# The last group's small pass evicted by two engines, and its two closings split between them

## The chip, the cores and the metric

The kernel runs on one core of a Trainium2 chip. The core has a matrix engine (TensorE, PE in the profile, with its weight loads shown apart as PEld), a vector engine (VectorE, DVE), a scalar engine (ScalarE, ACT), a general engine (GpSimd, POOL) and a queue engine (SyncE, SP). They run side by side, each working through its own instructions in order, and wait for each other by semaphores. Matmuls write into PSUM, an accumulator memory used here as eight banks of 512 floats per partition; ScalarE and VectorE move results from there to the main on-chip memory ("eviction"). The metric is the device time of one execution in microseconds, lower is better.

## The reference

```python
# attention part: a causal convolution of 7 taps along the sequence, softmaxed weights per head
w = softmax(weight, axis=-1)                        # 8 heads x 7 taps
out[b, s, h, g] = sum_k w[h, k] * x_pad[b, s + k, h, g]
# channel part, x = out, D = 192, hidden width 4 * 192 = 768
xn = (x - mean) / sqrt(var + 1e-6) * g_ln
y = x + relu(xn @ w_ch1) @ w_ch2
```

Shapes are x: 8 x 4224 x 192 in float32; the result has the same shape.

## The kernel before

Rows are cut into 18 groups (two small ones first); a full group is 128 partitions x 16 rows of 192 channels. For every group VectorE and ScalarE compute the convolution, VectorE transposes it in 32x32 blocks, and TensorE does the *up* stage (192 to 768, then relu) and the *down* stage (768 to 192). The normalisation's mean is folded into the weights, and its scale (`rstd`, computed by GpSimd) is applied after the down stage.

From group 3 on the up stage is `up_mixed`, which saves matmuls: it does a 2x2 block product with seven products instead of eight (Strassen-like), and adds and subtracts blocks around them. Its hidden features are cut in two passes. The *small* pass `one` covers one of three feature blocks (`n == 1`, 24 matmuls in a product, 1,024 results per partition); the *large* pass `two` covers the other two (`PAIR = 2`, 48 matmuls, 2,048 results). Two sets of four PSUM banks, X and Y, take turns: while TensorE fills one, the other is read. A product begins only when the earlier contents of its set have been read out. Within a bank, the columns hold `f` (which feature block of the pass, 256 columns each); `q` is the bank in the set.

Two helpers read a set. `evict` (L640 to L642) copies or rectifies it on ScalarE. `close` (L644 to L652) adds it to a block `c` that was evicted earlier: either VectorE adds directly from PSUM (L648), or ScalarE copies the set to a spare part and a DMA on GpSimd's queue adds that part to `c` (L609, by `add_by_dma`).

In a group that is not the last, pass two closes c11 in two halves by `f`, each by a ScalarE copy and a DMA, and c22 in one piece in the same way; VectorE is busy there with the next group's convolution. In the last group there is no next group, so both are closed by VectorE as a whole. c21 is closed by VectorE in every group.

`next(ahead)` between the two passes emits the finish of the previous group on VectorE (`finish_fast`, L897 and L899: sums and block transposes of the previous down stage into the tile `ot`). In the last group two scalings of that tile by `rstd` follow on VectorE (L709), each followed by two DMAs that add to the output (L925). `down_fast` then starts with products over c11, c21 and c22; its results are read by ScalarE (L841).

The order of the work is written by hand: each engine executes in the order of emission, and a framework inserts the semaphores that the data and the PSUM banks need.

Of the kernel before, what the change touches and what calls it, by code (L numbers as in the profile page):

```python
# [10 lines left out]
AF = mybir.ActivationFunctionType  # L11
ALU = mybir.AluOpType
# [4 lines left out]
def kernel(  # L17
# [29 lines left out]
    nc = tc.nc  # L47
# [35 lines left out]
    PAIR = NF // 2 - 1  # L83
    HJ = J // 2
# [9 lines left out]
    def rows_of_out(g, j1, j2):  # L94

        b, j0, n = groups[g]
        if b is not None:
            return [(slice(0, P), outr[b, :, (j0 + j1) * D : (j0 + j2) * D])]
        left = out[:, P * R : S].rearrange("b (p r) d -> b p (r d)", p=LP)
        return [  # L100
            (slice(LP * b, LP * b + LP), left[b, :, j1 * D : j2 * D]) for b in range(B)
        ]
# [22 lines left out]
    def take_set():  # L125
        i = (turn[0] + 3) // 4 * 4 % 8
        turn[0] = i + 4
        return all_banks[:, i : i + 4]
# [357 lines left out]
    def store_y(g, queue=nc.sync):  # L486
        n = groups[g][2]
        for ps, rows in rows_of_out(g, 0, n):
            queue.dma_start(out=rows, in_=y[g][ps, 0:n].rearrange("p j d -> p (j d)"))
# [118 lines left out]
    def add_by_dma(dst, src):  # L608
        nc.gpsimd.dma_start(out=dst, in_=src, accum_op=ALU.add)  # L609

    def up_mixed(g, ahead, pending):
# [3 lines left out]
        last = g + 1 == NG  # L615
# [7 lines left out]
        class Pass:  # L623
# [15 lines left out]

            def evict(self, banks, dst, relu=False, f=None):  # L640
                src = self.seen(banks, f)
                nc.scalar.activation(dst, src, AF.Relu) if relu else nc.scalar.copy(dst, src)  # L642

            def close(self, c, banks, part=None, f=None):  # L644


                if part is None:
                    nc.vector.tensor_tensor(c, c, self.seen(banks), op=ALU.add)  # L648
                    return
                self.evict(banks, part, f=f)  # L650
                whole = "p f q w -> p (f q w)"
                add_by_dma(c.rearrange(whole), part.rearrange(whole))  # L652
# [4 lines left out]
        def parts(pool, tag):  # L657

            room = pool.tile([P, J * D], F32, tag=tag, name=f"parts_{tag}{g}")
            return room.rearrange("p (f q w) -> p f q w", q=NQ, w=W)  # L660

        def act_scales(j1, j2):
            if not last:
                scale(g - 1, j1, j2)

        def taps_of_next(*args, **kw):
            if not last:
                conv(g + 1, *args, **kw)


        X, Y = take_set(), take_set()
        one, two = Pass(PAIR, FC, X, Y), Pass(0, PAIR, Y, X)
        p = one
# [18 lines left out]
        p = two  # L692
        rooms = parts(cpool, "cs"), parts(bpool, "tb")
        p.product(Y, a11, p.b11, True, False)
        p.evict(Y, p.c11)
        p.product(X, a12, p.b21)
        if last:
            p.close(p.c11, X)
        else:
            for f in range(PAIR):  # L700
                p.close(p.c11[:, f : f + 1], X, rooms[0][:, f : f + 1], f)
            if g == 3:
                store_y(g, nc.gpsimd)
        act_scales(0, 1)
        if last:

            for j1 in (0, HJ):
                part, factor = ots[g - 1][:, j1 : j1 + HJ], rstd[g - 1][:, j1 : j1 + HJ]
                nc.vector.tensor_tensor(  # L709
                    part, part, factor.unsqueeze(2).to_broadcast([P, HJ, D]), op=ALU.mult  # L710
                )
                add_to_out(g - 1, j1, j1 + HJ)
        p.product(Y, s2, p.t[0], False, False)
        p.evict(Y, p.c21)
        one.relu(one.c11)
# [3 lines left out]
        p.product(Y, s1, p.b12, False, False)  # L719
        taps_of_next(2, 5)  # L720
        taps_of_next(5, 6, heads=(0, H // 2))
        p.close(p.c22, Y, None if last else rooms[1][:, 0:PAIR])
        p.product(X, a22, p.t[2], False)
        for f in range(PAIR):
            p.relu(p.c11[:, f : f + 1])
# [8 lines left out]
        p.product(Y, s4, p.b22, False)  # L734
        p.evict(Y, p.c12, True)
        if last:
            p.relu(p.c22)
        lower_sum(g, range(PAIR))
        if last:

# [65 lines left out]
    def lower_sum(g, fs=range(FC)):  # L806

        a = of_products(g)
        if g in MIXED:
            for f in fs:  # L810
                nc.vector.scalar_tensor_tensor(
                    out=a[:, 1, 0, f], in0=a[:, 1, 0, f], scalar=0.0, in1=a[:, 0, 0, f],
                    op0=ALU.max, op1=ALU.subtract,
                )
        else:
            half_sum(g, (1, 0), (1, 0), (0, 0), ALU.subtract, fs)
# [99 lines left out]
    def add_to_out(g, j1, j2):  # L916
        if groups[g][0] is None:

            j1, j2 = (0, j2) if j2 == groups[g][2] else (0, 0)
        for ps, rows in rows_of_out(g, j1, j2) if j2 else ():  # L920
            src = ots[g][ps, j1:j2].rearrange("p j d -> p (j d)")
            step = 4 * D if groups[g][0] is not None else (j2 - j1) * D
            for d0 in range(0, (j2 - j1) * D, step):
                d1 = min(d0 + step, (j2 - j1) * D)
                nc.gpsimd.dma_start(out=rows[:, d0:d1], in_=src[:, d0:d1], accum_op=ALU.add)  # L925
# [65 lines left out]
    for g in range(NG):  # L991
        mixed, last = g in MIXED, g + 1 == NG
        if g + 2 < NG and g not in (1, 2, 3):
            load_x(g + 2)
        if mixed:
            work = up_mixed(g, ahead(g), pending)
            pending = iter(())
        else:
            up(g)
            work = []  # L1000
# [90 lines left out]
```

## Time and profile before

| | us |
|---|---|
| median of 4 runs | 957.55 |
| lowest, highest | 956.03, 958.65 |
| profiled execution, its own time | 957.56 |
| its span, first to last instruction | 955.5 |
| TensorE matmuls busy | 947.3 (99%) |
| VectorE busy | 891.0 (93%) |
| ScalarE busy | 696.6 (73%) |
| GpSimd busy | 336.9 (35%) |
| last group, small pass (weight loads) | 894.49 to 904.11 |
| last group, large pass | 904.11 to 922.78 |

A busy TensorE is not TensorE at its peak, since matmuls overlap; its weight loads show better when it had to wait. In a timeline row the first number is the start in us from the start of the span, the second the time from the first instruction of the row to the end of its last, then engine, source line, operation, what is written and read, the shape and the number of instructions; in brackets is the idle time of the engine before the row and what ended it.

### The profile page before, as it was taken

Reading aid. Unit: us, or ns where it says so; the run is one execution under the profiler, and the core shown is the slowest. Engines: PE = TensorE matmul, PEld = TensorE weight load, DVE = VectorE, ACT = ScalarE, POOL = GpSimd, SP = SyncE. Lnnn points to the kernel's source line nnn. Section 1 sums busy time; section 2 is a strip of 40 time slices with the busy share of each in tenths; the row PEclk is TensorE's granted clock in tenths of the full one; section 3 lists DMA queues with packets and bytes.
Section 4 is the critical chain, followed back from the end, with each engine's and each line's share of the span. In section 5 each row is a group of like instructions: output and inputs, shape, how many; then the busy total and the mean of one; then the engine's idle time right before and its main releaser. Section 6 shows DMA issues by size and latency. Waiting matters only on the chain.

```text
span 955.5 us, 37878 instructions
## 1 busy us (share of the span) xinstructions
PE 947.3 (99%) x16858; PEld 735.9 (77%) x16858; DVE 891.0 (93%) x1489; ACT 696.6 (73%) x1165; POOL 336.9 (35%) x472
## 2 busy tenths in 40 slices
PE   8999999999999999999999999999999999999998
PEld 6998896876869687787968778695877869586787
DVE  7999999999999999999999999999999999999757
ACT  6753678596877959687795968779696877967462
POOL 1158422623145141533227141442316332261310
PEclk9999999999999999999999999999999999999999
DMA  8359589689797988979697896969889696778251
GB/s 207 105 155 216 103 227 279 120 186 229 135 266 138 245 163 186 220 132 276 122 254 152 192 221 128 275 132 251 157 193 213 129 274 133 175 135 139 43 95 67
DMA packets 39544, 168.82 MB, mean 177 GB/s; under 512 B 4437, under 2 KB 8150, under 8 KB 33367
## 3 DMA queue, kind: packets, MB, share of 16 engines
q0 software_dynamic: 32576, 106.25, 60.0%
q1 hardware_dynamic: 6800, 60.16, 17.2%
q8 instruction: 132, 2.16, 0.9%
q14 instruction: 30, 0.25, 0.1%
q10 hardware_dynamic: 6, 0.00, 0.0%
HBM read 38.93 MB, written 50.33 MB: 93 GB/s over the span
## 4 chain that ended last, share of the span: by engine, by line
PE 97%; DVE 1%; DMA 1%; SPq 0%; issue 0%; ACT 0%; DVEq 0%
PE ps L533 49%; PE ps L835 44%; PE ps L772 4%; DMA xg<-in_x_dram 1%; DVE y L417 1%; DVE yt L428 0%; SPq L220 0%; SPq L215 0%; PE ps L357 0%; PE ps L354 0%; SPq L168 0%; ACT y L380 0%; DVE y L929 0%; DVEq L417 0%; DVEq L428 0%
## 5 line engine op out<-in xcount | busy, mean ns | idle before, releaser
L417 DVE SCALAR_TENSOR_TENSOR y<-xg,taps,y 128x384 f32<-128x384 f32 (+3 forms) x720 | 365.0, 581 | 3.3 <-DMA y<-room 1.4
L835 PE MATMUL ps<-room,w2sums 128*32 128x256 f32 (+2 forms) x4608 | 247.3, 371 | 0.0
L533 PE MATMUL ps<-yt,w 32*128 32x256 f32 (+2 forms) x4104 | 234.8, 378 | 1.0 <-DVE yt L428 1.0
L642 ACT COPY room<-ps 128x1024 f32<-128x1024 f32 (+1 forms) x135 | 175.0, 1297 | 77.8 <-PE ps L533 77.8
L533 PEld LDWEIGHTS ps<-yt,w 32*128 32x128 f32 x4104 | 204.1, 185 | 26.4 <-issue 9.0
L835 PEld LDWEIGHTS ps<-room,w2sums 128*32 128x32 f32 x4608 | 150.6, 110 | 90.6 <-ACT room L655 5.0
L835 PE MATMUL ps<-room,w 128*32 128x256 f32 (+2 forms) x3456 | 189.4, 371 | 0.0
L802 DVE TENSOR_TENSOR room<-room 128x1024 f32<-128x1024 f32 (+2 forms) x147 | 161.2, 1169 | 22.9 <-PE ps L835 15.0
L835 PEld LDWEIGHTS ps<-room,w 128*32 128x32 f32 x3456 | 112.0, 110 | 69.1 <-DVE room L648 5.0
L533 PE MATMUL ps<-ysums,w1sums 32*128 32x256 f32 x2160 | 125.3, 379 | 0.2 <-issue 0.2
L533 PEld LDWEIGHTS ps<-ysums,w1sums 32*128 32x128 f32 x2160 | 109.1, 185 | 11.2 <-ACT room L642 3.6
L925 POOL DMA_DIRECT2D out_dram<-ot x69 | 59.0, 942 | 159.0 <-ACT ot L914 102.3
L409 POOL DMA_DIRECT2D y<-tb x59 | 52.5, 1386 | 154.2 <-ACT room L841 110.2
L841 ACT COPY cs<-ps 128x256 f32<-128x256 f32 (+2 forms) x192 | 70.2, 368 | 45.3 <-PE ps L835 45.2
L655 ACT ACTIVATE room<-room 128x1024 f32<-128x1024 f32 (+1 forms) x89 | 92.6, 1072 | 1.0 <-DMA room<-parts_cs 1.0
L914 ACT ACTIVATE ot<-ot,r 128x192 f32<-128x192 f32 x224 | 91.0, 465 | 0.0
L380 ACT ACTIVATE y<-xg,taps 128x384 f32<-128x384 f32 (+3 forms) x141 | 73.1, 608 | 1.1 <-DMA xg<-in_x_dram 1.1
L448 DVE BATCH_NORM_STATS2 st<-y 128x6 f32<-128x192 f32 x264 | 70.1, 343 | 0.0
L841 ACT COPY room<-ps 128x256 f32<-128x256 f32 (+2 forms) x96 | 35.5, 369 | 46.2 <-PE ps L835 44.2
L398 ACT ACTIVATE tb<-xg,taps 128x384 f32<-128x384 f32 (+1 forms) x120 | 66.0, 628 | 0.0
L533 PE MATMUL ps<-yt,w1sums 32*128 32x256 f32 x1080 | 65.2, 380 | 0.0
L533 PE MATMUL ps<-ysums,w 32*128 32x256 f32 x1080 | 64.6, 376 | 0.0
(113 smaller groups left out, 911.0 us busy)
## 6 DMA issues: line engine op xcount, KB each, us to landing
xg<-in_x_dram SPq DMA_DIRECT2D x14, 2112.0 KB, 16.8
room<-room POOLq DMA_DIRECT2D x45, 512.0 KB, 5.1
out_dram<-ot POOLq DMA_DIRECT2D x59, 384.0 KB, 9.6
y<-tb POOLq DMA_DIRECT2D x58, 384.0 KB, 9.0
out_dram<-y SPq DMA_DIRECT2D x13, 1536.0 KB, 9.2
room<-parts_cs POOLq DMA_DIRECT2D x28, 512.0 KB, 6.8
room<-parts_tb POOLq DMA_DIRECT2D x14, 1024.0 KB, 7.6
xg<-in_x_dram POOLq DMA_DIRECT2D x1, 2112.0 KB, 13.5
```

What stands on the lines that cost most here:

```text
L380: nc.scalar.mul(y[g][:, 0:n, cs], xg[g][:, 0:n, cs], taps[:, h, 0:1])
L398: nc.scalar.mul(tb[g][:, 0:n, cs], xg[g][:, 1 : 1 + n, cs], taps[:, h, 1:2])
L417: nc.vector.scalar_tensor_tensor(out=y[g][:, 0:n, cs], in0=t[:, k : k + n, cs], scalar=taps[:, h, k : k + 1], in1=y[g][:, 0:n, cs], op0=AL ...
L448: nc.vector.bn_stats(out=sums[g][:, j, :], in_=y[g][:, j, :])
L533: nc.tensor.matmul(banks[:, q, i * w : i * w + w], right[rows, c, P * i : P * i + P], left[rows, :, c, :], start=(first and c == 0 and i = ...
L642: nc.scalar.activation(dst, src, AF.Relu) if relu else nc.scalar.copy(dst, src)
L655: nc.scalar.activation(c, c, AF.Relu)
L802: nc.vector.tensor_tensor(a[:, *dst, f], a[:, *left, f], a[:, *right, f], op=op)
L835: nc.tensor.matmul(dst[C * q : C * q + C, 0:w], right[:, f, C * c : C * c + C], left[:, f, q], start=(first and f == PAIR), stop=(f == PAI ...
L841: nc.scalar.copy(to[:, c], dst[:, 0:w].rearrange("p (j t) -> p j t", t=t))
L914: nc.scalar.mul(ots[g][:, j, :], ots[g][:, j, :], rstd[g][:, j : j + 1])
L925: nc.gpsimd.dma_start(out=rows[:, d0:d1], in_=src[:, d0:d1], accum_op=ALU.add)
```

## The change

Only the last group is touched. In pass `one`, each eviction is cut by banks: ScalarE takes banks 0 and 1 of the set, VectorE banks 2 and 3. In pass `two`, c11 and c22 are each closed in two halves by `f`: the first by VectorE's sum from PSUM, the second by a ScalarE copy into a part of `rooms[1]` and a DMA that adds it. The four output DMAs of the previous group are issued after the closing of c22 instead of after each scaling. The final rectification of c22 is cut in two by `f`.

```diff
             def evict(self, banks, dst, relu=False, f=None):
                 src = self.seen(banks, f)
+                if last and self.n == 1:
+                    near, far = [[v[:, :, q : q + 2] for v in (dst, src)] for q in (0, 2)]
+                    if relu:
+                        nc.scalar.activation(*near, AF.Relu)
+                        nc.vector.tensor_scalar_max(*far, 0.0)
+                    else:
+                        nc.scalar.copy(*near)
+                        nc.vector.tensor_copy(*far)
+                    return
                 nc.scalar.activation(dst, src, AF.Relu) if relu else nc.scalar.copy(dst, src)
...
                 if part is None:
-                    nc.vector.tensor_tensor(c, c, self.seen(banks), op=ALU.add)
+                    nc.vector.tensor_tensor(c, c, self.seen(banks, f), op=ALU.add)
                     return
...
         p.product(X, a12, p.b21)
-        if last:
-            p.close(p.c11, X)
-        else:
-            for f in range(PAIR):
-                p.close(p.c11[:, f : f + 1], X, rooms[0][:, f : f + 1], f)
-            if g == 3:
-                store_y(g, nc.gpsimd)
+        for f in range(PAIR):
+            part = (rooms[1][:, 0:1] if f else None) if last else rooms[0][:, f : f + 1]
+            p.close(p.c11[:, f : f + 1], X, part, f)
+        if g == 3:
+            store_y(g, nc.gpsimd)
         act_scales(0, 1)
         if last:
...
                 nc.vector.tensor_tensor(
                     part, part, factor.unsqueeze(2).to_broadcast([P, HJ, D]), op=ALU.mult
                 )
-                add_to_out(g - 1, j1, j1 + HJ)
...
-        p.close(p.c22, Y, None if last else rooms[1][:, 0:PAIR])
+        if last:
+            for f in range(PAIR):
+                p.close(p.c22[:, f : f + 1], Y, rooms[1][:, f : f + 1] if f else None, f)
+            for j1 in (0, HJ):
+                add_to_out(g - 1, j1, j1 + HJ)
+        else:
+            p.close(p.c22, Y, rooms[1][:, 0:PAIR])
...
         if last:
-            p.relu(p.c22)
+            for f in range(PAIR):
+                p.relu(p.c22[:, f : f + 1])
```

Lines of the changed kernel stand 9 to 13 higher in its profile: `close`'s sum is L657 there, ScalarE's copies L648 and L651, the finish L910 and L912.

## The prediction

> **What bounds the kernel now.** I read the page's busy shares and chain first, then the weight loader's timeline in the last group (its starts give TensorE's pace), then the timelines of ScalarE and VectorE in the same stretch, then the DMA issues.
>
> ```profile
> PE 947.3 (99%) x16858; PEld 735.9 (77%) x16858; DVE 891.0 (93%) x1489; ACT 696.6 (73%) x1165; POOL 336.9 (35%) x472
> PE 97%; DVE 1%; DMA 1%; SPq 0%; issue 0%; ACT 0%; DVEq 0%
> ```
>
> 97% of the chain that ends last is matmul time, so only holes in TensorE's stream are to be won or lost. Those of the last group's up stage (start in us, duration, idle time before it and its releaser):
>
> ```profile
> 894.49 2.47 PEld L533 LDWEIGHTS ps<-yt,w 32*128 32x128 f32 x48 [0.41 <-issue]
> 897.20 1.18 PEld L533 LDWEIGHTS ps<-ysums,w1sums 32*128 32x128 f32 x24 [0.24 <-ACT room L642]
> 901.34 1.18 PEld L533 LDWEIGHTS ps<-yt,w1sums 32*128 32x128 f32 x24 [0.26 <-ACT room L642]
> 904.11 5.06 PEld L533 LDWEIGHTS ps<-yt,w 32*128 32x128 f32 x96 [0.22 <-ACT room L642]
> 909.18 2.58 PEld L533 LDWEIGHTS ps<-ysums,w1sums 32*128 32x128 f32 x48
> 912.05 2.47 PEld L533 LDWEIGHTS ps<-ysums,w1sums 32*128 32x128 f32 x48 [0.29 <-DVE room L648]
> 914.53 2.58 PEld L533 LDWEIGHTS ps<-ysums,w 32*128 32x128 f32 x48
> 917.12 2.58 PEld L533 LDWEIGHTS ps<-yt,w1sums 32*128 32x128 f32 x48
> 919.98 2.47 PEld L533 LDWEIGHTS ps<-yt,w 32*128 32x128 f32 x48 [0.28 <-DVE room L648]
> ```
>
> The small pass (7 products of 24 matmuls) runs from 894.49 to 904.11, 9.62 us, with three waits for a ScalarE eviction. The large pass waits 0.29 us for VectorE's closing of c11 and 0.28 us for that of c22. Unhindered, 48 matmuls take 2.59 us (914.53 to 917.12), so 24 take 1.295.
>
> The two evicting engines there:
>
> ```profile
> 896.14 1.01 ACT L642 COPY room<-ps 128x1024 f32<-128x1024 f32 x1 [1.13 <-PE ps L533]
> 916.75 2.95 ACT L655 ACTIVATE room<-room 128x1024 f32<-128x1024 f32 x3
> 922.92 1.88 ACT L642 ACTIVATE room<-ps 128x2048 f32<-128x2048 f32 x1 [3.22 <-PE ps L533]
> 926.49 0.97 ACT L841 COPY cs<-ps 128x192 f32<-128x192 f32 x4
> ```
>
> ```profile
> 888.94 1.07 DVE L875 TENSOR_TENSOR cs<-cs,ps 128x256 f32<-128x256 f32 x3
> 895.97 0.94 DVE L897 TENSOR_TENSOR cs<-cs,room 128x768 f32<-128x768 f32 x1
> 899.79 1.90 DVE L899 STREAM_TRANSPOSE ot<-cs 128x512 f32<-128x512 f32 x3
> 909.71 2.29 DVE L648 TENSOR_TENSOR room<-room,ps 128x2048 f32<-128x2048 f32 x1 [8.02 <-PE ps L533]
> ```
>
> What to see: VectorE finishes the group before (L897, L899) from 895.97 to 901.69, in 5.72 us, and then idles 8.02 us until c11's closing. That idle time is where the change puts work. The DMAs of this part (median us from issue to landing):
>
> ```profile
> room<-room POOLq DMA_DIRECT2D x3, 512.0 KB, 4.6
> out_dram<-ot POOLq DMA_DIRECT2D x4, 384.0 KB, 8.2
> ```
>
> **The change part by part**, against the profiled execution: span 955.5 us, its own time 957.56, so 2.06 lie around the span; the median of the four runs, 957.55, is the same. All products stay and TensorE's order is unchanged, and so is every group but the last.
>
> *1. Small pass.* Each eviction of 1,024 elements becomes 512 on ScalarE and 512 on VectorE, in different banks. ScalarE's copies take 0.37 us for 256 (L841) and 1.01 for 1,024, so 0.59 for 512. VectorE has no copy out of PSUM in this trace; its sums out of PSUM take 0.41 us alone for 256 (groups view of L875) and 2.29 for 2,048, on a line 0.68 for 512. A set's products come two apart: with the loader ready 0.24 us before 897.20, an eviction that begins at 896.14 may last about 0.8 us before TensorE waits. 0.68 fits, 1.01 did not. At 1.295 a product the pass lasts 9.07 instead of 9.62: **−0.55** at most, 0 if VectorE's copy is as slow as the present one. I take −0.52, as 0.68 is nearer the sums' rows; the large pass begins at 903.59. The new waits of TensorE on VectorE go to separate queue entries; the trace has such entries in this line at 51 ns, beside matmuls. I take 0 (bounds 0 and 8 x 0.05 = 0.4).
>
> *2. What queues behind VectorE's halves.* The finish of the group before stands behind the seven halves in VectorE's order. Its 5.72 us no longer start at 895.97 but after the last half, at 904.35 − 0.52 + 0.68 = 904.51, and end at 910.23. The idle 8.02 us are used up. Who waits: c11's closing, due at 909.71 − 0.52 = 909.19. It starts 1.06 us late.
>
> *3. c11's closing.* The sum of 2,048 on VectorE (2.29) becomes a sum of 1,024 there and a copy of 1,024 on ScalarE that a DMA adds. The halves are the left and right columns of the *same* four banks. The built kernel's instruction list shows ScalarE's two such copies each waiting on VectorE, so I count them in series: a sum of 1,024 is 1.19 (the line from 0.41 to 2.29), then 1.01. Hence 910.25 to 911.44, then 911.5 to 912.5, and TensorE goes on with s3·t1 at 912.55. It would be ready at 909.18 − 0.52 + 2.58 = 911.24: a wait of 1.3 us for the 0.29 of before. Against 912.05 the stream now stands at **+0.5**; the small pass's gain is spent. Were the halves side by side, it would go on at 911.5, and the stream stand at −0.55.
>
> Here a page bears on it. The Trainium skill, "PSUM — Partial Sum Buffer", section "PSUM bank collisions raise a hardware error", says the compiler's scheduler keeps any two engines apart that touch the same bank and partition quadrant, reads against reads included. No row of before shows two engines reading one bank. By the rule the sum is the serial one (+0.5); by the 128x1024 and 128x2048 rows read as if both engines were free, it is −0.55.
>
> *4. c22's closing.* VectorE is free (after c11 come the two scalings, 3.42 us, to 914.9). Half a sum from 917.64 + 0.5 = 918.14 to 919.33, then ScalarE's copy to 920.4. TensorE, ready at 917.12 + 0.5 + 2.58 = 920.2, starts s4·b22 at 920.45 for 919.98 before: the wait is 0.25 instead of 0.28, **−0.03**. Side by side it would be 0.
>
> *5. Behind that copy on ScalarE.* Three rectifications (2.95 us) move from 916.75 to 920.4 and end at 923.35. Next is c12's eviction, due at 922.92 + 0.47 = 923.39, which TensorE waits for in its first product of the down stage (0.29 us at 924.85 in before). It just fits: 0, with 0.04 us of cover; each further tenth of delay costs a tenth. One of the three needs c11's DMA: issued at about 912.5, landing 4.6 us later by the median row and 9.3 by the slowest of the other parts' rows (parts_cs, 4.5 to 9.3), so at 917 to 922; needed at about 921.5. Taken as 0.
>
> *6. c22's second rectification* needs the new DMA, issued at 920.4, landing at 925.0 by the median (6.0 is the slowest of its kind here: 926.4; 9.3: 929.7). The single 1.90 us becomes two of about 1.05, ending at 927.4. The four copies behind (0.97) end at 928.4; the last frees the bank that the product of c22 overwrites at about 929.1 (144 matmuls from 925.69 in 5.82, half of it, plus 0.47). Cover 0.7 us; taken as 0, with +0.4 at a landing 7.1 us after issue as the point where it begins.
>
> *7. Outputs of the group before* move behind both part DMAs in POOL's queue: issued from 921.3 instead of 913.97. Four issues of 0.87 and 9.9 us at most to land (that line's slowest) end at about 934; their tile is next written at 941.09. Cover 7 us; nothing is queued behind them on POOL. SP's queue is not touched. 0. The two added part DMAs cost POOL 0.87 us each, hidden, since it then only waits.
>
> Sum: −0.52 + 1.02 (c11) − 0.03 = **+0.47**, so 957.56 + 0.5 = 958.0 us.
>
> **Rivals.**
> - *A. The halves of a closing run side by side* (the waits on VectorE release early). c11 leaves −0.55, c22 −0.28: 956.7 us. For it: both engines have room there. Against: the waits listed in 3.
> - *B. The small pass gains nothing* (VectorE's copies about 0.9 us, or queue entries count), while the late finish stays: +1.0, 958.6 us. Against: the sums' rows, 1.05 ns an element.
> - *C. Slower side: c22's DMA lands late.* With the outputs behind it or a slow landing of 9.3 us, it is there at 929.7; rectification and copies end at 931.7, and TensorE waits 2.6 us at 929.1: 958.0 + 2.6 = 960.6. It decides from 7.1 us after issue. For it: parts_cs has a median of 6.8. Against: those go two at once beside other traffic; here the three lone ones took 4.5, 4.6 and 6.0.
> - *D. The change does nothing* within the noise: every gain and loss is a few tenths, so this cannot be told from the forecast.
>
> **How the numbers follow.** Forecast 0.62, A 0.10, B 0.16, C 0.12. What a measurement of this kernel can tell from no change is about 0.2%, 1.9 us: faster means under 955.6, slower over 959.5. Forecast, A and B all lie within, C over. The four runs of before spread from 956.03 to 958.65, about 1.3 us to either side, which adds small chances beyond both bounds. Faster 0.03, same 0.83, slower 0.14. The range goes from A less a little spread (956.3) to between B and C (959.8).
>
> **What would show it.** Weight loads of the small pass with no wait for ScalarE and the large pass beginning near 903.6; L910 and L912 from about 904.5 instead of 895.97; VectorE's first half closing near 910.3; ScalarE's parts_tb copies starting just after VectorE's halves end; a wait of about 1.3 us of TensorE before s3·t1; c12's eviction at about 923.4 with next to no idle time before it; the lone part DMAs landing after 4.5 to 6 us. It would be wrong if ScalarE's and VectorE's halves overlap, if VectorE's finish starts early, or if TensorE waits in the down stage for a DMA.

## The result and the profile after

The changed kernel takes 958.86 us (median of 40 runs, 957.2 to 960.94) against 957.51 (60 runs of the kernel before, 955.52 to 959.79): a ratio of 1.0016 with a 95% interval of 1.0011 to 1.0020, so it is slower by about 1.5 us (1.1 to 1.9). The profiled execution took 959.24 us with a span of 957.0, before 957.56 with 955.5. The forecast was 958.0 in a range of 956.3 to 959.8, with 83% on "same", a change of less than about 0.2%; the measured 0.16% is inside both.

Executions differ by a few tenths to two us before the last group begins, in code that the change does not touch (the small pass's first weight load stands at 894.49 in before, at 894.98 in after, and between 892.62 and 895.77 in the experiments). So places in the last group are compared from that first load on. The weight loader's timeline in the changed kernel:

```profile
894.98 2.47 PEld L533 LDWEIGHTS ps<-yt,w 32*128 32x128 f32 x48 [0.41 <-issue]
897.47 2.58 PEld L533 LDWEIGHTS ps<-ysums,w1sums 32*128 32x128 f32 x48
902.65 6.46 PEld L533 LDWEIGHTS ps<-yt,w 32*128 32x128 f32 x120
909.12 2.58 PEld L533 LDWEIGHTS ps<-ysums,w1sums 32*128 32x128 f32 x48
912.89 2.47 PEld L533 LDWEIGHTS ps<-ysums,w1sums 32*128 32x128 f32 x48 [1.19 <-ACT parts_tb L651]
920.79 2.47 PEld L533 LDWEIGHTS ps<-yt,w 32*128 32x128 f32 x48 [0.26 <-ACT parts_tb L651]
923.60 1.78 PEld L848 LDWEIGHTS ps<-room,w 128*32 128x32 f32 x48 [0.33 <-DVE room L657]
932.36 0.29 PEld L848 LDWEIGHTS ps<-room,w 128*32 128x32 f32 x7
933.56 2.54 PEld L848 LDWEIGHTS ps<-room,w 128*32 128x32 f32 x64 [0.91 <-issue]
945.34 7.77 PEld L785 LDWEIGHTS ps<-w,kept 128*128 128x128 f32 x48 [0.30 <-issue]
```

The same two places of the down stage in the kernel before, the product that has the hole above and the first load of the kept rows:

```profile
931.54 2.89 PEld L835 LDWEIGHTS ps<-room,w 128*32 128x32 f32 x72
943.51 7.77 PEld L772 LDWEIGHTS ps<-w,kept 128*128 128x128 f32 x48 [0.30 <-issue]
```

Three things are to be seen. The small pass has no wait for ScalarE any more. The wait before s3·t1 has grown from 0.29 to 1.19 us and names ScalarE's copy. And there is a hole of 0.91 us in the down stage, after 7 loads of a product, where the loader waited for nothing that the profile shows ("issue"); the kernel before has no such hole there. From the first load, s3·t1 stands at 17.91 us (before 17.56), s4·b22 at 25.81 (25.49), the down stage at 28.62 (28.29) and the first load of the kept rows at 50.36 (49.02). That last stretch (called "the stretch" below) is 1.34 us longer: 0.33 in the up stage, 1.01 in the down stage.

How the late start of s3·t1 comes about, in VectorE's and then ScalarE's timeline of the changed kernel:

```profile
904.43 0.69 DVE L646 TENSOR_SCALAR room<-ps 128x512 f32<-128x512 f32 x1 [0.60 <-PE ps L533]
905.03 0.95 DVE L910 TENSOR_TENSOR cs<-cs,room 128x768 f32<-128x768 f32 x1
908.79 1.90 DVE L912 STREAM_TRANSPOSE ot<-cs 128x512 f32<-128x512 f32 x3
910.61 1.18 DVE L657 TENSOR_TENSOR room<-room,ps 128x1024 f32<-128x1024 f32 x1
918.47 1.22 DVE L657 TENSOR_TENSOR room<-room,ps 128x1024 f32<-128x1024 f32 x1 [3.35 <-PE ps L533]
```

```profile
904.37 0.60 ACT L645 ACTIVATE room<-ps 128x512 f32<-128x512 f32 x1 [0.65 <-PE ps L533]
911.82 1.01 ACT L651 COPY parts_tb<-ps 128x1024 f32<-128x1024 f32 x1 [2.97 <-DVE room L657]
919.73 1.01 ACT L651 COPY parts_tb<-ps 128x1024 f32<-128x1024 f32 x1 [1.99 <-DVE room L657]
923.74 1.88 ACT L651 ACTIVATE room<-ps 128x2048 f32<-128x2048 f32 x1
```

VectorE ends its last half eviction at 905.1, then finishes the group before, and starts c11's half at 910.61 with no idle time. ScalarE sits idle for 2.97 us and begins its half of c11 just after VectorE's ends (910.61 + 1.18 = 911.79). The two halves run one after the other, in c22 as well.

### The profile page after: what moved, and what is told of

It reads as the page before. It is cut to its first block, busy times and chain, and to the rows that moved or that the text cites. A ratio compares the mean times of both kernels' runs of the same rounds, so it can differ in the third digit from the quotient of the medians.

```text
span 957.0 us, 37896 instructions
## 1 busy us (share of the span) xinstructions
PE 949.1 (99%) x16858; PEld 738.1 (77%) x16858; DVE 893.1 (93%) x1496; ACT 695.8 (73%) x1168; POOL 340.9 (36%) x474
## 4 chain that ended last, share of the span: by engine, by line
PE 66%; DVE 1%; issue 0%; ACT 0%; DVEq 0%
PE ps L848 34%; PE ps L533 31%; PE ps L785 1%; DVE ot L912 0%; DVE cs L910 0%; DVE room L657 0%; ACT parts_tb L651 0%; DVE y L942 0%; DVE room L646 0%; DVEq L912 0%
## 5 line engine op out<-in xcount | busy, mean ns | idle before, releaser
L651 ACT COPY room<-ps 128x1024 f32<-128x1024 f32 (+1 forms) x129 | 168.9, 1310 | 72.3 <-PE ps L533 72.0
L664 ACT ACTIVATE room<-room 128x1024 f32<-128x1024 f32 x90 | 92.6, 1062 | 0.8 <-DMA room<-parts_cs 0.6
```

The source lines that it names most:

```text
L664: nc.scalar.activation(c, c, AF.Relu)
```

## The experiments

After the result two causes stood for the 1.5 us. *Up stage*: the late finish and the halves in series, worth 0.3. *Code*: the hole of 0.91 us. It lies where the four output DMAs now fill the DMA engines, and TensorE's code comes over the same engines: the trace shows packets of 16,384 bytes in the queue marked "instruction". That they are TensorE's is inferred from their number and pace: the page counts 132 of them for 16,858 matmuls, one for about 128, and where a matmul takes 40 ns without disturbance (e5 below) they come every 5.0 to 5.2 us, about 128 matmuls. In this part of the changed kernel they start at 914.03, 921.89, 931.30 and 934.74; the gap of 9.4 us opens with the first packets of the part and the outputs (922.5) and ends some 3 us before their last (934.5). The DMA queues of the changed kernel from 926 to 934 us:

```profile
q0 software_dynamic: 547, 1.49, 99.0%
q8 instruction: 1, 0.02, 0.8%
```

(packets, MB, share of 16 engines.) The traffic does not slow the loads as such: the 144 loads ahead of the hole take 5.82 us beside it, as in the kernel before. The rival was that the hole belongs to the new code or to c22's halves. Times and durations below that have no fence are read from the same traces.

Ratios are against runs of the kernel before made alongside. Those of e1, e3, e4, e5, e7 and e8 all have 1.000 within their intervals, so what these runs say of a few tenths of a microsecond rests on the stretch, read from one profiled execution each. The kernel before and e1, which moves the outputs alone, agree on it to 0.01 us.

**e1: the late outputs alone, in the kernel before.**

```diff
-                add_to_out(g - 1, j1, j1 + HJ)
...
         p.close(p.c22, Y, None if last else rooms[1][:, 0:PAIR])
+        if last:
+            nc.gpsimd.tensor_copy(wmax[:, 0:1], p.c22[:, 0, 0, 0:1])
+            for j1 in (0, HJ):
+                add_to_out(g - 1, j1, j1 + HJ)
```

> The kernel before, with one edit: the four output DMAs of the group before the last are issued behind the closing of c22 (held back by a one-element copy on GpSimd that reads c22) instead of behind the scalings. Theory (the outputs now crowd the DMA engines while TensorE's code is fetched, and TensorE runs out of code in the down stage): outputs issued from about 920.2 instead of 914.0, a 16 KB instruction packet delayed by 3 to 4 us, a hole of 0.5 to 1.0 us marked issue in the weight loads of the down stage, time about 0.9 us over before (ratio 1.0005 to 1.001). Rival (the outputs' place costs nothing, the whole 1.5 us is in the evictions and closings): no hole, ratio 1.000.

Measured: 956.92 us, ratio 0.9993 (0.9983 to 1.0003), stretch 49.02 us as in before, and no hole. The outputs were issued at 921.50, in place of 913.97, and the code packets were 922.36 and 930.68, 8.3 us apart. So the outputs' late place delays the packet but is not enough for a hole. This went against my expectation; the table behind e5 shows what else it takes.

**e2: the changed kernel with the outputs back behind the scalings.**

```diff
+                add_to_out(g - 1, j1, j1 + HJ)
...
-            for j1 in (0, HJ):
-                add_to_out(g - 1, j1, j1 + HJ)
```

> The changed kernel with the output DMAs back behind the two scalings. Theory (code fetch behind the outputs): the up stage stays as in the changed kernel (s4*b22 25.8 us after the small pass's first load), the hole of 0.91 us in the down stage goes, time 0.9 us under the changed kernel, about 958.0. The added DMA of c22 now stands behind the outputs and lands later than its 5.1 us; from about 6.5 us on ScalarE's rectification and then TensorE wait for it, which would give back up to 1 us. Rival (the hole comes from something else in the down stage, such as c22's halves): the hole stays, 958.9.

Measured: 959.88 us, ratio 1.0024 (1.0013 to 1.0035), stretch 51.16 us. The hole is gone, as the theory had it, but the price that it named only as a possibility is larger than the gain. ScalarE's timeline and the weight loader's:

```profile
928.98 1.06 ACT L664 ACTIVATE room<-room 128x1024 f32<-128x1024 f32 x1 [2.84 <-DMA room<-parts_tb]
```

```profile
930.95 2.76 PEld L847 LDWEIGHTS ps<-room,w2sums 128*32 128x32 f32 x72 [1.97 <-ACT cs L853]
```

c22's part DMA, issued at 920.62 behind the outputs (issued from 913.33 to 917.12), lands after 8.3 us instead of 5.1; the second rectification of c22 waits 2.84 us for it, the copies behind it come late, and TensorE waits 1.97 us for a bank. That is the mechanism of the prediction's rival C, with the outputs in front of the part instead of behind it. The total of the forecast for this run (958.0) was wrong by it.

**e3: the closings halved by banks instead of columns.**

```diff
+            def close_by_banks(self, c, banks, part):
+                src = self.seen(banks)
+                near, far = c[:, :, 0:2], c[:, :, 2:4]
+                nc.vector.tensor_tensor(near, near, src[:, :, 0:2], op=ALU.add)
+                part = part.rearrange("p o q w -> p (o q w)")
+                nc.scalar.copy(
+                    part.rearrange("p (f q w) -> p f q w", f=PAIR, w=W), src[:, :, 2:4]
+                )
+                add_by_dma(
+                    far.rearrange("p f q w -> p f (q w)"),
+                    part.rearrange("p (f w) -> p f w", f=PAIR),
+                )
...
+        if last:
+            p.close_by_banks(p.c11, X, rooms[1][:, 0:1])
...
-            for f in range(PAIR):
-                p.close(p.c22[:, f : f + 1], Y, rooms[1][:, f : f + 1] if f else None, f)
+            p.close_by_banks(p.c22, Y, rooms[1][:, 1:2])
```

> The changed kernel with c11 and c22 halved by banks instead of by columns: VectorE sums banks 0 and 1, ScalarE copies banks 2 and 3, the DMA adds that part. Theory (the column halves are held in series since they share banks): ScalarE's copies no longer wait for VectorE and start with TensorE's end (c11 at 14.3 us after the small pass's first load, c22 at 23.3); s3*t1 waits about 0.3 us for VectorE's late half instead of 1.19, s4*b22 does not wait; the up stage ends about 1.1 us earlier than in the changed kernel; the outputs and so the hole for code stay; about 957.8. Rival (the late finish alone makes the wait, or the two engines cannot read PSUM side by side): s3*t1 waits about as long as in the changed kernel, 958.9.

Measured: 957.13 us, ratio 0.9998 (0.9987 to 1.0008), stretch 48.63 us, 1.73 under the changed kernel. VectorE's and ScalarE's halves of c22 and ScalarE's of c11:

```profile
916.55 1.22 DVE L666 TENSOR_TENSOR room<-room,ps 128x1024 f32<-128x1024 f32 x1 [2.28 <-PE ps L533]
```

```profile
908.76 1.01 ACT L668 COPY parts_tb<-ps 128x1024 f32<-128x1024 f32 x1 [0.75 <-PE ps L533]
916.55 1.01 ACT L668 COPY parts_tb<-ps 128x1024 f32<-128x1024 f32 x1 [0.61 <-PE ps L533]
```

Both halves of c22 start at 916.55; ScalarE waits for TensorE alone. The loader's waits before s3·t1 and s4·b22 are gone, although VectorE's half of c11 still stood behind the finish (909.76); s3·t1 is the second half of this row:

```profile
908.27 5.20 PEld L533 LDWEIGHTS ps<-ysums,w1sums 32*128 32x128 f32 x96
```

The Trainium skill, "PSUM — Partial Sum Buffer", section "PSUM bank collisions raise a hardware error", says that two engines on different banks run clean while the scheduler keeps those on one bank apart. The two runs agree: for c11 ScalarE sits idle 2.97 us until VectorE's half ends in the changed kernel and waits for TensorE alone here, and TensorE's wait before s3·t1 goes from 1.19 us to none. The hole is still there:

```profile
931.11 2.58 PEld L862 LDWEIGHTS ps<-room,w 128*32 128x32 f32 x65 [0.49 <-issue]
```

**e4: the changed kernel with the small pass on ScalarE alone.**

```diff
-                if last and self.n == 1:
+                if False:
```

> The changed kernel with the small pass evicted by ScalarE alone, as before. Theory (the finish of the group before, queued behind VectorE's halves, holds up c11): the small pass takes 9.6 us instead of 9.1, VectorE finishes the group before from about 1.5 us after the pass's first load, c11's half starts with TensorE's end; s3*t1 stands at 17.5 us after the first load instead of 17.9, with a wait near 0.8 us; s4*b22 near 25.4; about 0.4 us under the changed kernel if the hole for code stays. Rival (the series of VectorE and ScalarE alone makes the wait, the finish does not matter): s3*t1 at 18.4, slower than the changed kernel by 0.5 us.

Measured: 957.74 us, ratio 1.0007 (0.9995 to 1.0019), stretch 49.99 us. The small pass takes 9.61 us again, VectorE finishes the group before at once, and c11's half waits for TensorE instead of for VectorE's queue. The loader's timeline (first load at 892.62):

```profile
910.15 2.47 PEld L533 LDWEIGHTS ps<-ysums,w1sums 32*128 32x128 f32 x48 [0.27 <-ACT parts_tb L651]
930.83 2.54 PEld L848 LDWEIGHTS ps<-room,w 128*32 128x32 f32 x64 [0.91 <-issue]
```

s3·t1 stands at 17.53, as the theory had it and not at the rival's 18.4; only its wait was misjudged (0.27, not 0.8, since the product before it also begins later). Splitting the small pass, which shortens that pass by about 0.6 us, therefore costs 0.38 at s3·t1 in the changed kernel. The same hole of 0.91 stays.

**e5: the changed kernel without the output DMAs.**

```diff
-            for j1 in (0, HJ):
-                add_to_out(g - 1, j1, j1 + HJ)
```

> The changed kernel without the four output DMAs of the group before the last (those rows of the output lack the second summand; the rest is computed). Theory (the late outputs, behind c22's added DMA, hold up the fetch of TensorE's code): the 16 KB instruction packets stay 5 to 8 us apart, the hole of 0.91 us in the down stage is gone, the stretch from the small pass's first load to the first load of the kept rows is 49.4 to 49.5 us instead of 50.36. Rival (the hole belongs to TensorE's code or to its new waits, whatever the DMAs do): the hole stays, 50.36 us.

Measured: 957.65 us, ratio 1.0005 (0.9997 to 1.0014), stretch 49.36 us. The down stage runs through, in the loader's timeline:

```profile
925.57 5.82 PEld L846 LDWEIGHTS ps<-room,w2sums 128*32 128x32 f32 x144
931.41 2.89 PEld L846 LDWEIGHTS ps<-room,w 128*32 128x32 f32 x72
934.34 5.82 PEld L846 LDWEIGHTS ps<-room,w2sums 128*32 128x32 f32 x144
```

The up stage is the changed kernel's (s3·t1 at 17.91), the code packets are 920.81, 926.43 and 931.61, at most 5.6 us apart, and 1.00 us of the stretch is gone. The rivals that the hole belongs to the code itself, or to c22's halves, fall: e5 keeps both.

Together with e1 this gives the condition. The starts of the delayed packet after the down stage's first load, and the holes:

```
kernel                    packet after down stage begins    hole
changed kernel            7.70 us                           0.91 us
e4                        7.57                              0.91
e3                        7.11                              0.49
e1                        6.62                              none
e5 (no outputs)           3.78                              none
```

The hole opens about 9.05 us into the down stage, in the changed kernel, in e3 and in e4 alike, and the loads go on 2.3 to 2.4 us after the packet's start. So in this code a packet that starts later than about 6.7 us in is too late (an estimate from the two figures). In e1 there is no part DMA of c22 in front of the outputs, and the packet starts 0.5 to 1.1 us earlier. It is not that e1's outputs are issued earlier: their first issue lies 2.56 us before the down stage there and 2.97 in e3, which has the hole. (e1's code is not the changed kernel's, so that the missing part DMA is the difference is argued, not shown.)

No run delays the code packet alone, so the packet as the link from outputs to hole is inferred from these times. One thing more in the traces supports it. Holes of the same kind stand in code that the change does not touch, in the kernel before too:

```profile
444.27 2.52 PEld L835 LDWEIGHTS ps<-room,w2sums 128*32 128x32 f32 x50 [0.50 <-issue]
```

A code packet starts 2.25 us before these loads, 8.5 us after the one ahead of it; in the profiled execution of the changed kernel the packets at this place are 7.2 us apart, and there is no hole. In the nine traces the down stages have 25 such holes of more than 0.2 us, and in each the loads go on 2.2 to 2.6 us after a code packet's start. The Trainium skill, "Runtime: NRT & Kernel Launch", section "Instruction fetch mechanics", states that code comes in blocks of 16 KiB over a DMA queue and that crossing a block is mostly hidden. The packets' size agrees, and these runs show places where it was not hidden.

**e8: the split of the small pass alone, in the kernel before.** Its edit is the first hunk of the change (`evict`) and nothing else.

> The kernel before with the small pass split between the two engines and nothing else changed: closings whole on VectorE, outputs behind the scalings. Theory (in the changed kernel c11's halves in series take as long as a whole sum, and the late finish is what costs): small pass 9.0 us, c11's sum starts at 15.6 us after the first load, behind the finish, lasts 2.29; s3*t1 at 17.9, as in the changed kernel; s4*b22 at 25.8; no hole; the stretch 49.35 us, 0.3 over the kernel before, ratio 1.0003. Rival (halving pays, and the DMAs of the parts are what costs): s3*t1 later than in the changed kernel by 0.3 us or more.

Measured: 957.77 us, ratio 1.0003 (0.9995 to 1.0012), stretch 49.39 us, no hole. VectorE's and then the loader's timeline (first load at 893.93):

```profile
909.56 2.25 DVE L657 TENSOR_TENSOR room<-room,ps 128x2048 f32<-128x2048 f32 x1
```

```profile
911.86 2.47 PEld L533 LDWEIGHTS ps<-ysums,w1sums 32*128 32x128 f32 x48 [1.21 <-DVE room L657]
919.79 2.47 PEld L533 LDWEIGHTS ps<-yt,w 32*128 32x128 f32 x48 [0.28 <-DVE room L657]
```

s3·t1 at 17.93 and s4·b22 at 25.86, within 0.05 us of the changed kernel's: halving a closing by columns is worth nothing, because its halves in series take as long as the whole sum.

**e7: what the runs point to.** The small pass split, c11 halved by banks, c22 whole on VectorE, outputs behind the scalings as before. The edit is against the changed kernel, with `close_by_banks` as in e3.

```diff
+        if last:
+            p.close_by_banks(p.c11, X, rooms[1][:, 0:1])
...
+                add_to_out(g - 1, j1, j1 + HJ)
...
-        if last:
-            for f in range(PAIR):
-                p.close(p.c22[:, f : f + 1], Y, rooms[1][:, f : f + 1] if f else None, f)
-            for j1 in (0, HJ):
-                add_to_out(g - 1, j1, j1 + HJ)
-        else:
-            p.close(p.c22, Y, rooms[1][:, 0:PAIR])
+        p.close(p.c22, Y, None if last else rooms[1][:, 0:PAIR])
```

> The small pass split as in the changed kernel, c11 halved by banks, c22 closed by VectorE as a whole as before, outputs issued behind the scalings as before. Theory: small pass 9.0 us, no wait before s3*t1, 0.28 us before s4*b22, no hole and no wait for a DMA in the down stage; the stretch from the small pass's first load to the first load of the kept rows 48.35 us, 0.67 under the kernel before, ratio about 0.9993. Rival (the outputs' old place also holds up TensorE's code once c11's DMA stands before them): a hole of 0.5 to 1 us around 924 to 928, stretch 49 or more.

Measured: 956.97 us, ratio 0.9996 (0.9987 to 1.0004), stretch 48.39 us: no wait before s3·t1, 0.28 us before s4·b22, no hole. In the last group it is 0.63 us shorter than the kernel before (0.67 forecast). c11's part, cut by banks, takes 7.3 us to land (7.2 in e3, 4.8 by columns in the changed kernel), and ScalarE waits 1.47 us for it in the up stage, but TensorE does not. Its total time cannot be told apart from before.

## Why the prediction was right or wrong

The direction and the range held; the size was a third of the measured one. That the range held is in part luck: its upper end came from rivals B and C, which did not occur, and three quarters of the stretch's 1.34 us came from a step that was taken as 0. By its steps:

1. *Small pass*, −0.52: right in kind, too small. VectorE's copy of 512 took 0.69 us (estimate 0.68), ScalarE's 0.59 (0.59). The pass took 8.97 us: the seventh product's loads begin at 902.65, a product is 1.295. That is 0.65 less than before, more than the "at most" of 0.55: seven products of 1.295 were too long, since the first two together took 2.49 and not 2.59.
2. *The finish behind the halves*: right. c11's sum started 15.63 us after the first load (15.76 by the working), with no idle time before it. e3 and e8 show that the finish alone does not decide: with the halves by banks it is hidden, with the whole sum TensorE waits the 1.21 us.
3. *c11 in series*, stream at +0.5: right in kind, measured +0.35, with a wait of 1.19 (1.3). The line from 0.41 to 2.29 gives 1.22 for a sum of 1,024, not the 1.19 written; measured were 1.18 and 1.22. Rival A fell here: the copies did wait for VectorE, and only other banks (e3) let them run side by side.
4. *c22*: wait 0.26 (0.25); the stream stands at +0.32 (+0.47).
5. *Three rectifications before c12*: right. c12's eviction starts at 923.74 with no idle time, and TensorE's wait stayed 0.29.
6. *c22's part DMA*: landed after 5.1 us, no wait (4.6 to 6.0 by the rows). Rival C did not occur in the changed kernel. e2 shows that it occurs with the outputs in front, and what it costs: 1.97 us at a landing of 8.3 us, so the wait begins at about 6.3 us (an estimate from the two), earlier than the 7.1 of the working.
7. *Outputs moved, taken as 0*: this step failed. It counted the cover only to the tile's next write at 941.09 and did not look at what else travels on the DMA engines. Moving the outputs behind the part put 1.5 MB, with the part's 0.5 MB in front, into the time from 922 to 934 us, mostly the down stage, and a packet of TensorE's code came too late: 0.91 us (e5: 1.00 us of the stretch). The sign that the prediction gave, a wait of TensorE in the down stage for a DMA, came in this form: the transfer was one of code, and the profile names no releaser. Leaving the outputs in place was no way out: with c22's part behind them it cost 1.97 us (e2).

In the up stage the sum was +0.47 and is +0.33; in the down stage it was 0 and is +1.01. The stretch's 1.34 us lies within the interval of the timed difference, 1.0011 to 1.0020 of 957.5, or 1.1 to 1.9 us. Rival B (+1.0 in the up stage) did not occur.

## What to carry to other kernels

When two engines share an eviction, cut it by PSUM banks; a cut inside a bank is put in series by the semaphores and gains nothing. When an idle engine is given work in front of an existing queue, ask what stood behind that idle time: here the finish, moved back, used it up and held up the next closing. And a bulk transfer that is moved to a "free" stretch needs a look at all the traffic of that stretch, the code packets included; here the last group's holes lay in the down stage, where the matmuls are short. An idle time marked "issue" in the middle of a product is a reason to look at when the last code packet started.

## What the hardware showed that I had not expected

In the kernel before, the code packets around the outputs are 10.6 us apart (913.26 and 923.86), more than the 9.4 of the changed kernel, without a hole. A long gap alone is thus not enough: each trace has 14 to 20 gaps of over 9 us between code packets, and most of them have no hole. In the kernel before this gap lies in the up stage, at 54 ns a matmul (48 in 2.59 us); in the down stage a matmul takes 40 (144 in 5.82), so code is used up faster. The delay itself is also smaller there: measured against the gaps of e5, which lacks the outputs, 7.6 us at the first place and 5.6 at the second, it is about 3.0 us in the kernel before and 3.8 in the changed one. Which of the two decides is not shown; both are worked out from these figures, and no run tests one alone.

In the changed kernel, four DMAs behind c22's part thus cost about 1 us by way of a 16 KB packet that no instruction of the kernel asks for.
